# The cosine half of a folded Fourier mixing: rows combined from the tiles just filled instead of a reload, and the turning transfers spread

## The chip, the core and the metric

The kernel runs on one core of a Trainium2 chip. The metric is the device time in microseconds (us) of one execution, from the chip's own clock; several executions give a median. Engines are named as in the profile: PE (TensorE matmul), PEld (its weight loads), DVE (VectorE), ACT (ScalarE), POOL (GpSimd), SP (SyncE, which issues nearly all transfers). "L994" is line 994 of the kernel before; the changed kernel's lines stand about 3 (before the combining) or 24 (behind it) further down.

## What is computed

Two independent things, laid side by side in the output. With S = 2048 and D = 448:

```python
# half A: Fourier mixing with given DFT matrices
a = einsum("bsd,ed->bse", x, dft_hid_re)
b = einsum("bsd,ed->bse", x, dft_hid_im)
y = einsum("ts,bse->bte", dft_seq_re, a) - einsum("ts,bse->bte", dft_seq_im, b)
# half B: attention with 16 heads of 28
q, k, v = split(x_b @ wqkv)
o = softmax(q @ k.T * 28**-0.5) @ v @ wo
out = concatenate([y, o], axis=-1)
```

## The kernel before, in words

**Two streams on one PE.** Attention makes 1024 score tiles of 128x512 (`score`, matmul L1451), whose exponential on ACT (L1455) goes into tiles of the pool `kept_s` (20 tiles of 128x2x512, fp32), and blocks that multiply the exponentials with V (PV, L1462, 32 matmul rows each). All else on PE is filler that goes between scores: projections (L653) first, then the feature transform of half A (`hidden_both`, L886, matmul L908), then the sequence transform in two parts, cosine and sine (`sequence_halved`, matmul L1192), then the output projection (L1686, L1717).

**How the order is made.** A planner in Python (`Schedule`, L124 to L330) writes out the order of all five engines. A task has a key (its due time), a planned duration, tasks that it depends on and slots that it takes from pools. On each engine the ready task with the smallest key is taken; `hold=True` keeps a transfer back until the filler has come to its key. The real engines run their queues in that order, so a waiting instruction holds back all that stand behind it. Three numbers of the planner appear in the change: `RUN` (how many half products, `MZ`, go in a row before something else may), `NOTE_AT` (how early a check's reduction is due) and `FAR_LATE` (how late a store of the far rows is due). Where PE would stand idle in the plan, a score may be emitted twice, to keep PE fed (the repeat writes the same values to the same bank).

**The feature transform.** For each of eight pairs of row tiles, in the order `PAIRS_AT = (7, 0, 6, 1, 5, 2, 4, 3)`, the folded input is split into high and low parts (L873, L879, L881), multiplied (L908), and copied from PSUM into a tile `pair` of `kept_s` by three copies (L504 on DVE or L502 on ACT). `pair` holds for one tile of rows both parts, cosine ([:, 0]) and sine ([:, 1]). It is stored to DRAM, `ab_d` (L917). With rows reversed, it is copied from DRAM to DRAM into `turned_ab` (`turn_rows`, L959: one small copy L974 and four of 32 rows or fewer L969 for each of four groups).

**Combining.** `combine(part, at, after)` (L980) makes the operands of the sequence transform for each part. `group(g)` loads the group's two tiles from `ab_d` into a slot x (L987) and the turned ones into m (L990), casts the low columns of x into `zt` (L994, the z products' operand), makes the sum and difference of the two tiles of x into y (L996) and of m back into x (L998), combines both (L1001) and casts them into the room for `u` (L1003, L1004). `plain(h)` loads a pair of tiles that have no turned partner (L1011) and casts its low columns only (L1015). `combine(0, ...)` is for the cosine part and is called while the feature transform is under way; `combine(1, ...)` is called for the sine part, behind the cosine part's sequence stage.

**Other instructions that stand in the same queues.** `tops(g)` (L1421) makes a product of the first keys (L1435), transposes it on DVE (L1438, which frees its PSUM bank), reduces it (L1439), transposes the result (L1442) and stores it (L1444). The output of a PV block is normalised on DVE (L1517 to L1521) and stored (L1527). Differences of rows for the sequence stage are made on DVE (L1226, L1230, L1235), sums for checks by L1140, L1146 and L1148; weights are loaded by L1164 and L955; q and k by L1313, L1314.

Of the kernel before, what the change touches and what calls it, by code (L numbers as in the profile page):

```python
# [26 lines left out]
NT = S // P  # L27
# [36 lines left out]
NOTE_AT = 5  # L64
# [4 lines left out]
FAR_LATE = 15  # L69
# [3 lines left out]
TURN_LEAD = 18  # L73
# [23 lines left out]
RUN = 8  # L97
# [259 lines left out]
def tile_kernel(ctx, tc, xa, wre, wim, wd, xb, wqkv, wo, out):  # L357
# [461 lines left out]
    def halves(t):  # L819
        return t.rearrange("p (a b) -> p a b", a=2)  # L820
# [67 lines left out]
    def hidden_both(ready):  # L888
        for g in PAIRS_AT:
            x, ld = rows_both(g, fkey(0, 0) - 13)  # L890
            for a in range(2):
# [13 lines left out]
                for b, (seq, o) in enumerate(((seq, fill_s.slot()), (rest, fill_s.slot()))):  # L905
                    for n, (w, i, y, c0, c1, d) in enumerate(seq):
                        def emit(e, w=w, i=i, y=y, c0=c0, c1=c1, o=o, n=n, m=len(seq) - 1):
                            nc.tensor.matmul(o.t[:, c0:c1], of(w, i), y(), start=n == 0, stop=n == m)  # L908
                        last[0] = pe(at, emit, d=d, deps=[last[0], *([h, *ready] if n == 0 else [l] if n == 1 else [])],
                                     use=[hi, lo, o, *low_in, *([pair] if n == len(seq) - 1 else [])])  # L910
                        at += d
                    ways = ((0, 0, EVEN), (1, EVEN, 2 * MAIN)) if b == 0 else ((None, 0, 2 * REST),)
                    for e, c0, c1 in ways:
                        to = lambda pair=pair, e=e: tight(pair.t)[:, :, MAIN:D] if e is None else tight(pair.t)[:, :, e:MAIN:2]
                        ends.append(sch.add({"ACT": 0.43 if e is None else 0.3, "DVE": 0.53 if e is None else 0.32}, key - 10,
                                            lambda w, o=o, to=to, c0=c0, c1=c1: copy_of(w, to(), halves(o.t[:, c0:c1])), deps=[last[0]], use=[o, pair]))
                ab_done[st] = dma(key - 10, lambda pair=pair, st=st: nc.sync.dma_start(  # L917
                    ab_d[st % HT][st // HT].rearrange("b p d -> p b d"), tight(pair.t)), 448, -1.5, deps=ends, use=[pair])

    ab_done, g_at = {}, {}  # L920
# [7 lines left out]
    def z_of(t):  # L928
        return zt()[:, t * LOW:(t + 1) * LOW]
# [29 lines left out]
    def turn_rows(at):  # L959
# [4 lines left out]
        for g in range(FT):  # L964
# [6 lines left out]
            ab_turned[g, 2] = [dma(at(g), lambda n=n, put=put: put(n), 224, 1.5, each=0.75, deps=[ab_done[far], ab_done[far + HT]]) for n in range(4)]  # L971
            if g:
                def first(g=g):
                    nc.sync.dma_start(rows_at(turned_ab[g], 0, [[P * D, 4], [1, D]]), rows_at(ab_d[HT - g], 0, [[P * D, 4], [1, D]]))  # L974
                ab_turned[g, 0] = [dma(at(g), first, 7, 1.5, deps=[ab_done[HT - g], ab_done[NT - g]])]
# [4 lines left out]
    def combine(part, at, after):  # L980
        half = lambda s, i, n=D: tight(s.t)[:, i, :n]
        minus, plus = (ALU.add, ALU.subtract) if part else (ALU.subtract, ALU.add)

        def group(g):
            key = at(g)
            x, y, m = kept_s.slot(), kept_s.slot(), kept_s.slot()
            ld = dma(key, hold=True, emit=lambda: nc.sync.dma_start(tight(x.t), of_rows(ab_d[g], part)),  # L987
                     size=448, extra=0.3, deps=[ab_done[g], ab_done[g + HT]], use=[x])
# [3 lines left out]
            zs = []  # L992
            for j in range(2):
                zs.append(dve(key, lambda j=j: nc.vector.tensor_copy(z_of(g + j * HT), half(x, j, LOW)), 0.26, deps=[ld, *after(g)], use=[x]))  # L994
                z_ready[part, g + j * HT] = zs[j]
            us = [dve_on(key, lambda e, c=c, op=op: e.tensor_tensor(half(y, c), half(x, 0), half(x, 1), op=op), 0.6, deps=[ld], use=[x, y])  # L996
                  for c, op in enumerate((ALU.add, ALU.subtract))]
            ws = [dve_on(key, lambda e, c=c, op=op: e.tensor_tensor(half(x, c), half(m, 0), half(m, 1), op=op), 0.6,  # L998
                         deps=[lm, *us, *zs], use=[x, m]) for c, op in enumerate((ALU.add, ALU.subtract))]
# [8 lines left out]
        def plain(h):  # L1008
            key = at(h) + 1
            x = kept_s.slot()  # L1010
# [810 lines left out]
```

## Time and profile before

| what | us |
|---|---|
| median of three timed runs (lowest, highest) | 798.53 (798.12, 799.5) |
| the profiled execution | 797.17 |
| its span, first to last instruction | 795.4 |
| PE busy | 779.8 (98%) |
| ACT busy | 590.7 (74%) |
| DVE busy | 439.6 (55%) |
| mean granted clock of PE | 0.997 |

The profile shows one execution; the span is 1.77 us shorter than its time. Filler and attention change with the stage: in the trace, projections and values run to about 225 us, the feature transform to about 403, the cosine part to about 575, the sine part to about 705, the output projection to 789. A share of busy time is an average over these stages. A wait in the lists is given as total us, times and the longest, with the instruction that waited and the one that released it.

### The profile page before, as it was taken

What the parts mean: (1) busy time and instruction counts of PE and PEld (TensorE: products, weight loads), DVE (VectorE), ACT (ScalarE), POOL (GpSimd) and SP (SyncE); (2) the same over time, 40 slices, a digit from 0 to 9 for tenths busy, and PEclk for the clock granted to TensorE, in tenths of its full rate; (3) what the DMA queues carried; (4) which work ended last, traced back from release to release, by engine and by line L of the source; (5) the groups of instructions that cost most, each with busy time, mean ns of one, the idle gap of its engine ahead of it and who ended that gap; (6) DMA issues with size and microseconds to landing.
All of it is one profiled execution on the core that took longest, in us unless ns stands there. A gap on an engine that the chain in (4) does not pass through costs nothing.

```text
span 795.4 us, 14120 instructions
## 1 busy us (share of the span) xinstructions
PE 779.8 (98%) x4725; PEld 482.9 (61%) x4725; DVE 439.6 (55%) x928; ACT 590.7 (74%) x1221; POOL 55.9 (7%) x201
## 2 busy tenths in 40 slices
PE   8999999999999989999999999999999999999996
PEld 6886556575556646556566555556555555655576
DVE  6641443362243463444559775679887876673440
ACT  6105877568787868887888878988778888899941
POOL 3000000000000000000011110122011202010000
PEclk9999999999999999999999999999999999999999
DMA  8757876342357554556578875696877849763132
GB/s 297 216 175 236 233 199 215 123 181 102 116 108 223 166 173 135 167 162 208 187 232 244 260 224 169 200 300 180 235 253 245 265 142 290 225 218 116 33 136 86
DMA packets 138610, 152.58 MB, mean 192 GB/s; under 512 B 31140, under 2 KB 109538, under 8 KB 138530
## 3 DMA queue, kind: packets, MB, share of 16 engines
q1 hardware_dynamic: 137810, 150.46, 61.4%
q10 hardware_dynamic: 720, 1.15, 0.4%
q8 instruction: 39, 0.64, 0.4%
q14 instruction: 41, 0.34, 0.1%
HBM read 110.39 MB, written 50.86 MB: 203 GB/s over the span
## 4 chain that ended last, share of the span: by engine, by line
PE 84%; DMA 8%; SPq 3%; ACT 2%; DVE 2%; issue 1%; DVEq 0%
PE bank L1451 29%; PE bank L1462 26%; PE bank L653 11%; PE bank L1192 8%; PE bank L1686 4%; PE bank L908 4%; ACT kept L1455 2%; DMA abd<-kept 1%; DMA kept<-wre 1%; DMA wraw<-wre 1%; DMA k<-qkd 1%; DMA abt<-abd 1%; PE bank L1717 1%; DMA kept<-wqkv 1%; PE bank L1435 1%
## 5 line engine op out<-in xcount | busy, mean ns | idle before, releaser
L1455 ACT ACTIVATE kept<-bank 128x512 f32<-128x512 f32 x1024 | 511.1, 664 | 147.6 <-PE bank L1451 138.1
L1451 PE MATMUL bank<-q,k 85*128 85x512 f32 x1028 | 340.7, 415 | 5.3 <-DVE kept L1438 2.8
L1451 PEld LDWEIGHTS bank<-q,k 85*128 85x128 f32 x1028 | 181.4, 189 | 104.2 <-issue 30.8
L1462 PE MATMUL bank<-kept,v 128*32 128x512 f32 x2048 | 233.0, 595 | 0.0
L1462 PEld LDWEIGHTS bank<-kept,v 128*32 128x32 f32 x2048 | 60.0, 109 | 133.4 <-issue 128.3
L504 DVE COPY kept<-bank 128x226 f32<-128x226 f32 (+3 forms) x64 | 30.8, 503 | 79.2 <-PE bank L908 46.2
L653 PE MATMUL bank<-xt,whi 128*128 128x512 f32 x196 | 69.1, 399 | 1.6 <-DVE xt L498 0.8
L1192 PE MATMUL bank<-zt 128*128 128x226 bf16 x448 | 55.3, 262 | 0.4 <-DVE zt L1226 0.3
L1148 DVE TENSOR_REDUCE diff<-zt 128x1 f32<-128x512 bf16 x73 | 47.7, 677 | 1.1 <-POOL zt L1245 0.7
L1192 PEld LDWEIGHTS <-zt 128*128 128x128 bf16 x448 | 38.4, 99 | 15.0 <-issue 11.3
L653 PEld LDWEIGHTS bank<-xt,whi 128*128 128x128 f32 x196 | 36.4, 188 | 13.7 <-DVE xt L498 1.8
L653 PE MATMUL bank<-xt,wlo 128*128 128x512 f32 x112 | 43.8, 393 | 0.0
L908 PE MATMUL bank<-wd,whi 128*128 128x450 f32 (+3 forms) x128 | 43.0, 381 | 0.0
L653 PE MATMUL bank<-wd,xt 128*128 128x448 f32 x176 | 37.7, 368 | 0.6 <-DVE wd L498 0.6
L1192 PE MATMUL bank<-xt,whi 128*128 128x448 f32 (+1 forms) x128 | 38.2, 326 | 0.0
L653 PEld LDWEIGHTS bank<-wd,xt 128*128 128x128 f32 x176 | 32.7, 188 | 4.6 <-POOL wlo L640 1.0
L1517 DVE STREAM_TRANSPOSE kept<-bank 128x512 f32<-128x512 f32 (+1 forms) x19 | 13.5, 713 | 32.1 <-PE bank L1462 22.7
L504 DVE CAST wd<-bank 128x512 fp32r<-128x512 f32 x12 | 8.3, 691 | 40.6 <-PE bank L653 39.2
L502 ACT ACTIVATE kept<-bank 128x448 f32<-128x448 f32 (+2 forms) x17 | 9.9, 584 | 27.2 <-PE bank L1717 14.8
L1235 DVE TENSOR_TENSOR zt<-wdraw,xraw 128x508 bf16<-128x508 f32 x28 | 19.1, 683 | 17.0 <-PE bank L1192 9.1
L1146 ACT ACTIVATE spent<-zt 128x512 uint8<-128x512 bf16 x39 | 26.0, 666 | 3.3 <-DVE zt L1226 2.0
L1192 PEld LDWEIGHTS bank<-xt,whi 128*128 128x128 f32 x128 | 24.6, 197 | 3.7 <-ACT kept L1455 1.3
(168 smaller groups left out, 742.1 us busy)
## 6 DMA issues: line engine op xcount, KB each, us to landing
wdraw<-wim SPq DMA_DIRECT2D x38, 256.0 KB
qkd<-wd SPq DMA_DIRECT2D x32, 256.0 KB
wdraw<-wre SPq DMA_DIRECT2D x32, 256.0 KB
q<-qkd SPq DMA_DIRECT2D x64, 112.0 KB
k<-qkd SPq DMA_DIRECT2D x64, 112.0 KB
abd<-kept SPq DMA_DIRECT2D x16, 448.0 KB
kept<-abd SPq DMA_DIRECT2D x16, 448.0 KB
qkd<-kept SPq DMA_DIRECT2D x24, 256.0 KB
```

What stands on the lines that cost most here:

```text
L504: nc.vector.tensor_copy(dst, src)
L653: nc.tensor.matmul(o.t[:, :cols], w(), x(), start=(i == 0), stop=(i == n - 1))
L908: nc.tensor.matmul(o.t[:, c0:c1], of(w, i), y(), start=n == 0, stop=n == m)
L1146: nc.scalar.activation(spent, src(), AF.Abs, accum_out=dst)
L1148: nc.vector.tensor_reduce(dst, src(), axis=AX.X, op=ALU.add, apply_absolute_value=True)
L1192: nc.tensor.matmul(o.t[:, at0:at0 + n], cut_of(w.t, e, c), x(), start=first, stop=stop)
L1235: e.tensor_tensor(turned(dl.t, 1, 1, P - 1), mirror(r.t), read(base.t, 1, 1, P - 1), op=minus)
L1451: m = pe(key, lambda e: nc.tensor.matmul(b.t, KT[h][kt // 4].t[:KR + 1, kt % 4 * P:(kt % 4 + 1) * P], q.t[:KR + 1, :], start=True, stop=True),
L1455: return act(key - 20, lambda: nc.scalar.activation(p.t, b.t, AF.Exp, scale=SCALE), deps=[m], use=[b, pair])
L1462: nc.tensor.matmul(o.t[j * VW:(j + 1) * VW, :], VT[h].t[:, kt // 4, kt % 4, :], tiles[i // 2].t[:, i % 2, :], start=(kt < 4 // len(cs)), s ...
L1517: t = dve(key - 20, lambda: nc.vector.transpose(pair.t[:m, 0], o.t[:m]), 0.66, deps=[dep], use=[o, pair], own=RAW_S)
L1686: nc.tensor.matmul(o.t[:, :D], a(), b(), start=(i == 0), stop=(i == 8 and n < N_HELD))
```

## The change

It does four things. (1) In the cosine part, z and the first sums are made straight from the pair tiles that `hidden_both` filled; nothing is loaded from `ab_d` for it. The pair tiles are remembered in `pairs`, and stay taken until the sums have read them and their store has landed. The turned rows are loaded as before, and their sum and difference no longer wait for the sums of the pair. (2) The turning copies are spread by 3 us of due time, due 22 instead of 18 us ahead, planned as 448 instead of 224 KB, and held. (3) The pair's store is planned with 0 instead of −1.5 us extra. (4) `RUN`, `NOTE_AT` and `FAR_LATE` are changed. The sine part combines as before, from reloads.

```diff
-NOTE_AT = 5
+NOTE_AT = 4
-FAR_LATE = 15
+FAR_LATE = 5.0
-TURN_LEAD = 18
+TURN_LEAD = 22
+TURN_STEP = 3.0
+OWN_LEAD = 0.0
+AB_EXTRA = 0.0
-RUN = 8
+RUN = 7
...
+                pairs[st] = pair, ends, key - OWN_LEAD
                 ab_done[st] = dma(key - 10, lambda pair=pair, st=st: nc.sync.dma_start(
-                    ab_d[st % HT][st // HT].rearrange("b p d -> p b d"), tight(pair.t)), 448, -1.5, deps=ends, use=[pair])
+                    ab_d[st % HT][st // HT].rearrange("b p d -> p b d"), tight(pair.t)), 448, AB_EXTRA, deps=ends, use=[pair])
...
-            ab_turned[g, 2] = [dma(at(g), lambda n=n, put=put: put(n), 224, 1.5, each=0.75, deps=[ab_done[far], ab_done[far + HT]]) for n in range(4)]
...
-                ab_turned[g, 0] = [dma(at(g), first, 7, 1.5, deps=[ab_done[HT - g], ab_done[NT - g]])]
+                ab_turned[g, 0] = [dma(at(g) - TURN_STEP, first, 7, 2.5, each=0.6, deps=[ab_done[HT - g], ab_done[NT - g]])]
+            ab_turned[g, 2] = [dma(at(g) + n * TURN_STEP, lambda n=n, put=put: put(n), 448, 1.5, each=0.75, hold=True,
+                                   deps=[ab_done[far], ab_done[far + HT]]) for n in range(4)]
...
+        def own(t, after):
+            pair, ends, key = pairs[t]
+            z_ready[part, t] = dve(key, lambda: nc.vector.tensor_copy(z_of(t), half(pair, part, LOW)), 0.26, deps=[*ends, *after], use=[pair])
+
         def group(g):
...
+            if part == 0:
+                for j in range(2):
+                    own(g + j * HT, after(g))
+                src = [pairs[g + j * HT][0] for j in range(2)]
+                ld = [d for j in range(2) for d in pairs[g + j * HT][1]]
+                of = lambda j: half(src[j], part)
+                zs = []
+            else:
+                of = lambda j: half(x, j)
+                src = [x]
+                ld = [dma(key, hold=True, emit=lambda: nc.sync.dma_start(tight(x.t), of_rows(ab_d[g], part)),
+                          size=448, extra=0.3, deps=[ab_done[g], ab_done[g + HT]], use=[x])]
...
-            us = [dve_on(key, lambda e, c=c, op=op: e.tensor_tensor(half(y, c), half(x, 0), half(x, 1), op=op), 0.6, deps=[ld], use=[x, y])
+            us = [dve_on(key, lambda e, c=c, op=op: e.tensor_tensor(half(y, c), of(0), of(1), op=op), 0.6, deps=ld, use=[*src, y])
...
-                         deps=[lm, *us, *zs], use=[x, m]) for c, op in enumerate((ALU.add, ALU.subtract))]
+                         deps=[lm, *(us if part else ()), *zs], use=[x, m]) for c, op in enumerate((ALU.add, ALU.subtract))]
...
         def plain(h):
             key = at(h) + 1
+            if part == 0:
+                for j in range(2):
+                    own(FT + h + j * HT, after(h))
+                return
```

How the order of the engines moves is shown at three places. `kept`, `bank`, `zt`, `xt` and the like are tiles; the number behind a name tells tiles of one pool apart; `abd` and `abt` are `ab_d` and `turned_ab` in DRAM.

The first place is DVE's queue at the first group of the cosine part, in the middle of the feature transform (about 280 us in the trace of before). Before:

```order
L504 COPY kept_239<-bank_264 128x2x223
L879 TENSOR_SCALAR whi_203<-wraw_200 128x512
L881 SCALAR_TENSOR_TENSOR wlo_204<-wraw_200,whi_203 128x512
L873 TENSOR_TENSOR wraw_200<-kept_226 128x256 x2
L994 CAST zt<-kept_231 128x226 x2
L996 TENSOR_TENSOR kept_243<-kept_231 128x448 x2
L998 TENSOR_TENSOR kept_231<-kept_241 128x448 x2
L1438 STREAM_TRANSPOSE kept_232<-bank_270 128x512
L1001 TENSOR_TENSOR kept_243<-kept_243,kept_231 128x448
L1439 TENSOR_REDUCE kept_232<-kept_232 128x16
```

After (L507 is the copy L504 of before, L1016 the sums L996, L991 the casts to z, L882, L884 and L876 the splits, L1018 the sums of the turned rows L998, L1021 the combining L1001):

```order
L507 COPY kept_229<-bank_265 128x2x223
L1016 TENSOR_TENSOR kept_241<-kept_237,kept_229 128x448 x2
L991 CAST zt<-kept_229 128x226
L882 TENSOR_SCALAR whi_202<-wraw_199 128x512
L884 SCALAR_TENSOR_TENSOR wlo_206<-wraw_199,whi_202 128x512
L876 TENSOR_TENSOR wraw_199<-kept_228 128x256 x2
L507 COPY kept_238<-bank_267 128x2x113
L507 COPY kept_238<-bank_267 128x2x112
L1018 TENSOR_TENSOR kept_231<-kept_245 128x448 x2
L1021 TENSOR_TENSOR kept_241<-kept_241,kept_231 128x448
L1023 CAST xt_193<-kept_241 128x448
```

The casts and the sums stand right behind the copies that fill their tiles; the sums of the turned rows stand by themselves, later, and the transpose of the tops (L1462 there) follows 22 rows behind them.

The second place is SP's queue at the same group. Before:

```order
L1313 DMA k_211<-qkd 56x1x512
L1314 DMA k_211<-qkd 28x512
L990 DMA kept_241<-abt_176 128x2x448
L955 DMA basd_180<-wre 8x15x512
L917 DMA abd_168<-kept_243 128x2x448
L987 DMA kept_231<-abd_168 128x2x448
L1164 DMA xraw<-basd_180 128x2x256 x2
```

After (L973 and L977 are the turning copies L969 and L974 of before, L921 the store L917, L959 the table's turning L955, L1009 the load of turned rows L990):

```order
L973 DMA abt_176<-abd_175 4x32x448
L1468 DMA md_140<-top_252 128x32
L921 DMA abd_168<-kept_237 128x2x448
L973 DMA abt_176<-abd_175 4x32x448 x2
L973 DMA abt_176<-abd_175 4x31x448
L959 DMA basd_180<-wre 8x16x512
L977 DMA abt_177<-abd_175 4x448
L1337 DMA k_211<-qkd 56x1x512
L1338 DMA k_211<-qkd 28x512
L921 DMA abd_168<-kept_229 128x2x448
L959 DMA basd_180<-wre 8x15x512
L1009 DMA kept_245<-abt_176 128x2x448
```

The reload L987 behind the store is gone, and the turning copies stand with other transfers between them. In the whole program there are 8 loads from `abd` of a pair (L987 and L1011) where there were 16.

The third place is PE's queue where the cosine part's filler ends and the sine part's begins (about 570 us in the trace of before). Before:

```order
L1451 MATMUL bank_265<-q_223,k_210 128x512
L1192 MATMUL bank_264<-xt_194,whi_203 128x226
L1192 MATMUL bank_264<-xt_194,wlo_208 128x226
L1451 MATMUL bank_271<-q_220,k_210 128x512
L1451 MATMUL bank_269<-q_221,k_210 128x512
L1451 MATMUL bank_270<-q_222,k_210 128x512
L1451 MATMUL bank_265<-q_223,k_210 128x512
L1451 MATMUL bank_271<-q_220,k_210 128x512 x2
L1451 MATMUL bank_269<-q_221,k_210 128x512 x2
L1192 MATMUL bank_267<-xt_194,whi_203 128x448
```

After, the last eleven rows of the run and the first of the PV block behind it (L1475 is the score, L1486 PV):

```order
L1475 MATMUL bank_268<-q_219,k_212 128x512
L1475 MATMUL bank_270<-q_216,k_212 128x512 x2
L1475 MATMUL bank_271<-q_217,k_212 128x512 x2
L1475 MATMUL bank_266<-q_218,k_212 128x512 x2
L1475 MATMUL bank_269<-q_219,k_212 128x512 x2
L1475 MATMUL bank_268<-q_216,k_213 128x512 x2
L1475 MATMUL bank_270<-q_217,k_213 128x512 x2
L1475 MATMUL bank_264<-q_218,k_213 128x512
L1475 MATMUL bank_271<-q_219,k_213 128x512
L1475 MATMUL bank_266<-q_216,k_213 128x512
L1475 MATMUL bank_269<-q_217,k_213 128x512 x2
L1486 MATMUL bank_268<-kept_243,v_214 32x512 x2
```

A run of eight scores (six and two repeats; a score row with "x2" is a score and its repeat) between products becomes a run of 25 (18 and seven repeats) between two PV blocks, with four scores and another seven z products behind the second.

More of the change, by code (lines that the diff above doesn't have):

```diff
@@ L916, in hidden_both @@
                                             lambda w, o=o, to=to, c0=c0, c1=c1: copy_of(w, to(), halves(o.t[:, c0:c1])), deps=[last[0]], use=[o, pair]))
+                pairs[st] = pair, ends, key - OWN_LEAD
                 ab_done[st] = dma(key - 10, lambda pair=pair, st=st: nc.sync.dma_start(
-                    ab_d[st % HT][st // HT].rearrange("b p d -> p b d"), tight(pair.t)), 448, -1.5, deps=ends, use=[pair])
-    ab_done, g_at = {}, {}
+                    ab_d[st % HT][st // HT].rearrange("b p d -> p b d"), tight(pair.t)), 448, AB_EXTRA, deps=ends, use=[pair])
+    ab_done, g_at, pairs = {}, {}, {}
     u_ready, z_ready, u_last = {}, {}, {}
@@ L986, in group @@
             x, y, m = kept_s.slot(), kept_s.slot(), kept_s.slot()
-            ld = dma(key, hold=True, emit=lambda: nc.sync.dma_start(tight(x.t), of_rows(ab_d[g], part)),
-                     size=448, extra=0.3, deps=[ab_done[g], ab_done[g + HT]], use=[x])
+            if part == 0:
[10 more added lines that the diff above has]
+                          size=448, extra=0.3, deps=[ab_done[g], ab_done[g + HT]], use=[x])]
             lm = dma(key + 1, hold=True, emit=lambda: nc.sync.dma_start(tight(m.t), of_rows(turned_ab[g], part)),
                      size=448, extra=0.3, deps=[d for n in (0, 2) for d in ab_turned[g, n]], use=[m])
[L992 to L996, printed above, removed]
+            if part:
+                zs = []
+                for j in range(2):
+                    zs.append(dve(key, lambda j=j: nc.vector.tensor_copy(z_of(g + j * HT), half(x, j, LOW)), 0.26, deps=[*ld, *after(g)], use=[x]))
+                    z_ready[part, g + j * HT] = zs[j]
+            us = [dve_on(key, lambda e, c=c, op=op: e.tensor_tensor(half(y, c), of(0), of(1), op=op), 0.6, deps=ld, use=[*src, y])
                   for c, op in enumerate((ALU.add, ALU.subtract))]
             ws = [dve_on(key, lambda e, c=c, op=op: e.tensor_tensor(half(x, c), half(m, 0), half(m, 1), op=op), 0.6,
-                         deps=[lm, *us, *zs], use=[x, m]) for c, op in enumerate((ALU.add, ALU.subtract))]
+                         deps=[lm, *(us if part else ()), *zs], use=[x, m]) for c, op in enumerate((ALU.add, ALU.subtract))]
             for c, op in enumerate((plus, minus)):
@@ L1009, in plain @@
             key = at(h) + 1
+            if part == 0:
+                for j in range(2):
+                    own(FT + h + j * HT, after(h))
+                return
             x = kept_s.slot()
```

## The prediction, on record before the run

> **What bounds the kernel now.** I read the head of the page first, then what TensorE (PE) waited for, then the chain of waits around the largest of those waits, and last the same stretch in short windows with the granted clock. The head of the page and the top of PE's waits:
>
> ```profile
> span 795.4 us, 14120 instructions
> PE 779.8 (98%) x4725; PEld 482.9 (61%) x4725; DVE 439.6 (55%) x928; ACT 590.7 (74%) x1221; POOL 55.9 (7%) x201
> ...
> PE bank L1451 <- DVE kept L1438: 2.8, 1, 2.8
> PE bank L1545 <- POOL ident masks.py:199: 1.4, 1, 1.4
> ```
>
> PE is busy in 98% of the span, so what can be won is little: its idle time (795.4 − 779.8 = 15.6 us, much of it the start and the drain), the time in which it runs at a lower clock, and the time in which a row counts as busy but is stretched because ScalarE (ACT) can't empty banks faster. The largest wait of PE in the whole run is a single one of 2.8 us: a score (L1451) that needs a PSUM bank, which the transpose L1438 on VectorE (DVE) frees. The chain of waits through that place:
>
> ```profile
> 274.76 5.69 DMA abd<-kept
> ...
> 280.53 0.03 SPq L987
> ...
> 280.60 3.54 DMA kept<-abd
> ...
> 284.16 0.04 DVE zt L994
> ...
> 284.63 1.08 DVE kept L996 x2
> ...
> 285.73 1.16 DVE kept L998 x2
> 286.89 0.64 DVE kept L1438
> ...
> 287.57 0.73 PE bank L1451 x2
> ```
>
> Read from the bottom: the score waits for L1438; L1438 has nothing to do with the combining, but stands behind L994, L996 and L998 in DVE's queue; L994 stands there waiting for the reload of a pair from DRAM (3.54 us); and that reload waited on SP's queue for the landing of the pair's own store (5.69 us). So a round trip of 9.2 us through DRAM holds a PSUM bank back. PE's timeline and the short windows (per engine busy us and count, then the granted clock, DMA share, GB/s) price it:
>
> ```profile
> 282.82 1.34 PE L1451 MATMUL bank<-q,k 85*128 85x512 f32 x5
> 284.00 0.27 PE L908 MATMUL bank<-wlo,whi 128*128 128x226 f32 x1
> ...
> 287.57 0.73 PE L1451 MATMUL bank<-q,k 85*128 85x512 f32 x2 [2.84 <-DVE kept L1438]
> ```
>
> ```profile
> 284.00:286.00 2.00, 0.73 (x4) 0.30 (x2) 1.80 (x5) 2.00 (x5) 0.20 (x1) 1.00 1.05 335
> 286.00:288.00 2.00, 0.43 (x2) 0.39 (x3) 2.00 (x5) 0.31 (x1) 0.00 (x0) 1.00 0.75 269
> 288.00:290.00 2.00, 2.00 (x11) 1.75 (x10) 1.97 (x7) 1.83 (x4) 0.00 (x0) 0.79 0.35 86
> 290.00:292.00 2.00, 2.00 (x7) 1.72 (x7) 1.42 (x5) 1.64 (x4) 0.00 (x0) 0.50 0.43 109
> 292.00:294.00 2.00, 2.00 (x14) 1.17 (x16) 1.31 (x3) 1.28 (x4) 0.00 (x0) 0.86 0.67 171
> ```
>
> PE stands for 2.84 us, and behind the wait the granted clock is 0.79, 0.50 and 0.86 in three windows of 2 us: 2 x (0.21 + 0.50 + 0.14) = 1.70 us of full-speed work lost. The whole stall costs 2.84 + 1.70 = 4.54 us.
>
> A sentence on the clock from outside the rows: the Trainium skill, "TensorE: Matmul & The Clock Gate", section "Part 1: The HAM clock gate", has the clock halve after at least one idle window of about 3.4 us, the window running freely; taken as a threshold on the gap, a wait of 2.84 us would cost no clock, the saving would be 2.84 and the sum below 1.70 us smaller. The trace shows the half clock after 2.84 us of idling, so the measurement decides, and 1.70 us stands.
>
> **The change part by part.** 1. *No reload in the cosine half.* The casts to z and the two sums of each group now read the pair tiles that were just filled. Four L987 and four L1011 issues of 448 KB go from the SP queue, and with them what L994 waited for and what L987 waited for on SP (a row of the list of waits, then two of SP's own list: us in total, times, longest):
>
> ```profile
> DVE zt L994 <- DMA kept<-abd: 6.4, 3, 3.9
> ...
> SPq L990 <- DMA abt<-abd: 18.0, 5, 5.2
> ...
> SPq L987 <- DMA abd<-kept: 12.8, 4, 5.3
> ```
>
> In the new order the casts and sums stand right behind the copies that fill their tiles, and the next transpose of the kind of L1438 stands over 20 rows behind the last instruction that waits for a load. The 2.84 us wait and its clock loss go: −4.54 us. The other two waits of L994 (6.4 − 3.9 = 2.5 us) had no PE wait behind them in the list above and bring nothing. What is late next at this place is the row pair L998, which still waits for the turned rows that come by store, turning copy and load; it now waits without L996 in front of it. I put it at zero, since L998 began right behind L996 in the chain (its load was there already), and price its failure among the rivals.
>
> 2. *Issues and bytes.* Eight loads less are off the path, since SP's queue stood waiting anyway (18.0 and 12.8 us in the rows above): zero. If the transfers of that stretch get faster by it, nothing but a wait that is already priced gets shorter: zero.
>
> 3. *Turning copies spread, stores planned later.* The copies of a group now go out with 3 us between them in the plan, a lead of 22 instead of 18 and twice the planned size. Their end decides when L990 can load and L998 run. They move behind other loads in the SP queue, and are held until the filler work has come that far. Transfers of this kind took between 3.54 us and the two below, so the plan's margin may fail by some us: zero in the forecast, a rival below.
>
> ```profile
> 343.94 4.88 DMA abd<-kept
> ...
> 349.98 6.91 DMA abt<-abd
> ...
> 356.95 8.78 DMA wraw<-wre
> ```
>
> 4. *The start of the sine half.* This is the price of the change that I can see. The three numbers of the planner (notes, far differences, runs of half products) and the different use of the slots move the filler there. In before, PE had one run of eight scores at this place (six scores and two that are repeated, since the planner puts a repeat where PE has nothing else), then product and score in turn. In the new order there is a run of 25 between two blocks of PV: 18 scores and 7 repeats. A run without filler goes at ACT's pace, once the banks are used up. ACT's timeline and PE's at that place:
>
> ```profile
> 570.87 9.91 ACT L1455 ACTIVATE kept<-bank 128x512 f32<-128x512 f32 x20 [3.01 <-PE bank L1451]
> ```
>
> ```profile
> 573.70 2.96 PE L1451 MATMUL bank<-q,k 85*128 85x512 f32 x8
> 576.50 0.36 PE L1192 MATMUL bank<-xt,whi 128*128 128x448 f32 x1
> ```
>
> An exponential takes 9.91 / 20 = 0.50 us; a score on PE takes (284.00 − 282.82) / 5 = 0.236. PE's excess in the old run was 576.50 − 573.70 − 6 x 0.236 = 1.38 us. In the new one the first six scores find banks (the block of PV ahead gives ACT time to catch up), and the other twelve are paced by ACT: 12 x (0.50 − 0.236) = 3.17 us, in which the 7 repeats (7 x 0.236 = 1.65 us) fit. The difference is 3.17 − 1.38 = +1.8 us. Lower bound: if the planner's repeats are all that is lost, 5 more repeats in the whole program x 0.236 = 1.18 in all; upper bound: all 18 at ACT's pace, 18 x 0.264 − 1.38 = +3.4 us. I take 1.8, from the row of the run that is nearest in kind.
>
> 5. *The start of the cosine half.* A run of nine scores with two repeats appears where there was none: 2 x 0.236 = +0.5 us (between 0, if ACT had to catch up anyway, and the 1.38 of the old run).
>
> 6. *The tail.* With 18 scores drawn forward at one place, 1001 of the scores (repeats counted) are out by the end of the sequence stage, 951 before. The stretch in which ACT was the end of the chain before that point:
>
> ```profile
> 700.92 5.00 ACT kept L1455 x10
> ...
> 706.97 0.50 PE bank L1451
> ```
>
> gets easier, and the output projection keeps fewer runs of six to eight scores (one for four). Between 0 and the 1.38 us that one such run cost: I take −0.5 us.
>
> 7. *Copies from DVE to ACT* (about five) and one sum moved between them: ACT is busy 590.7 of 795.4 us and the move is some 2 us of it, hidden at 74%; zero, or inside part 4 where it isn't hidden.
>
> Sum: −4.54 + 1.8 + 0.5 − 0.5 = −2.74 us. The profiled execution took 797.17 us (span 795.4 and 1.77 around it), so 794.43. The median of the three timed runs is 798.53, 1.36 above the profiled one; the forecast on that scale is 798.53 − 2.74 = **795.8 us**. With the bounds of parts 4 to 6 it lies between 794.2 and 797.
>
> **The rivals.** (a) *The runs cost nothing.* If ACT's time ahead of schedule in the long run is given back in full later, parts 4 and 5 vanish and the time is 798.53 − 4.54 − 0.5 = 793.5 us. For it: the number of exponentials is the same, and scores drawn forward leave PE's later filler free. Against it: PE is the bound over the span, and an ACT-paced run is PE time that no later stage returns. Chance 0.17.
>
> (b) *The wait comes back at the turned rows: no change.* L998 is now the first DVE instruction of the group that waits for DRAM; behind it stand splits of the weights, copies that free banks and the transposes. If its turned rows come as late as L990's longest wait on SP (5.2 us in the rows above), PE stands again for about the 2.84 us: 795.8 + 2.84 = 798.6 us without a clock loss, 800.3 with one of 1.70. For it: 18.0 us of SP's waiting is for the turning copies, and these are now spread out. Against it: the longer lead, and L998 found its rows ready in before. Chance 0.20.
>
> (c) *Slower, at the start of the sine half.* All four groups and the plain casts of the sine half now stand on DVE ahead of the next differences that feed PE. One group with its plain casts took 576.95 − 571.16 = 5.79 us on DVE:
>
> ```profile
> 571.16 0.46 DVE L994 CAST zt<-kept 128x226 bf16<-128x226 f32 x2
> ...
> 576.95 0.41 DVE L1083 CAST xt<-kept 96x512 fp32r<-96x512 f32 x1
> ```
>
> Two groups and about 1 us of other work stand between the products around the long run, 12.6 us; PE's cover is that run (6 x 0.236 + 12 x 0.50 = 7.4), two blocks of PV of 3.6 us as below, and eight scores (1.9): 16.5 us. A margin of 3.9 us.
>
> ```profile
> 278.67 3.64 PE L1462 MATMUL bank<-kept,v 128*32 128x512 f32 x32
> ```
>
> It decides from the point where the reloads (which the sine half still makes) are late by more than that: one that takes 8.78 instead of 3.54 us is late by 5.2 and costs 1.3 us; two in a row are late by 10.5 and cost 6.6. Halfway, 4 us, with the clock loss of 1.70, gives 795.8 + 5.7 = 801.5 us. For it: each reload is in front of everything on an in-order queue, and that stretch is rich in transfers. Against it: two late transfers must meet. Chance 0.13.
>
> **How the numbers follow.** The forecast has 0.50, (a) 0.17, (b) 0.20, (c) 0.13. A measurement of this kernel can tell about 0.2%, 1.6 us: faster is below 796.9, slower above 800.1. Faster: 0.45 of the forecast and (a)'s 0.17, 0.61 with rounding down for the upper edge. Same: the rest of the forecast and most of (b), 0.23. Slower: (c) and the part of (b) with a clock loss, 0.16. The range reaches from within (a), 792.4, to the top of (b), 800.4, and leaves out (c) and the lower part of (a), under 2 in 10.
>
> **What would show it right or wrong.** In the changed profile the wait of a score for the transpose of the tops should be gone from the top of PE's waits, and the granted clock should be 1.00 from 284 to 296 us; SP should hold four loads of pairs where it held eight, and no cast of the cosine half should wait for a load. The run of 25 should show as some 7.4 us of scores with ACT behind ACT without a gap. A PE wait on DVE in the feature stage with a chain over turning copies is (b); a PE wait of over 2 us for z or differences near 570 to 600 us is (c). If the long stall is gone and the time is still within 0.2%, part 4 was mis-sized; if PE's rows show neither wait nor stretch there, it is (a).

## The result, and the profile after

| kernel | median us (lowest, highest; runs) | ratio to before, 95% interval |
|---|---|---|
| before | 798.53 (796.99, 801.14; 6) | |
| after | 793.25 (792.91, 794.62; 6) | 0.9929 [0.9907, 0.9951] |

The change makes the kernel 5.3 us faster. The forecast was −2.7 us, to 795.8; the time lies inside its range, and next to rival (a)'s 793.5. The profiled executions differ by less than the medians: 797.17 before, 793.73 after, −3.4 us. The head of the page of after and the top of PE's waits:

```profile
span 791.9 us, 14113 instructions
PE 780.8 (99%) x4730; PEld 481.0 (61%) x4730; DVE 440.2 (56%) x921; ACT 593.0 (75%) x1227; POOL 54.9 (7%) x201
...
PE bank L1569 <- POOL ident masks.py:199: 1.4, 1, 1.4
PE bank L656 <- ACT xt L595: 1.1, 1, 1.1
```

The wait of 2.8 us for the transpose of the tops is gone; PE's longest wait is now one at the start of the program. The windows at the place where it was (columns as in the prediction):

```profile
284.00:286.00 2.00, 2.00 (x12) 1.64 (x10) 1.69 (x6) 2.00 (x6) 0.00 (x0) 1.00 0.36 86
286.00:288.00 2.00, 2.00 (x11) 1.60 (x11) 1.90 (x5) 2.00 (x6) 0.00 (x0) 1.00 0.55 171
288.00:290.00 2.00, 2.00 (x19) 0.64 (x21) 0.65 (x2) 2.00 (x6) 0.00 (x0) 1.00 0.54 135
290.00:292.00 2.00, 2.00 (x21) 0.48 (x13) 0.00 (x0) 0.61 (x2) 0.00 (x0) 1.00 0.83 277
```

PE is busy throughout and the granted clock stays at 1.00, as it does up to 296 us. DVE's, SP's and PE's timelines at the other two places that the prediction speaks of:

```profile
278.36 1.16 DVE L1018 TENSOR_TENSOR kept<-kept 128x448 f32<-128x448 f32 x2 [3.06 <-ACT kept L1479]
```

```profile
272.91 0.36 SPq L1009 DMA_DIRECT2D kept<-abt  x1
```

```profile
579.23 7.31 PE L1475 MATMUL bank<-q,k 85*128 85x512 f32 x25
586.47 3.64 PE L1486 MATMUL bank<-kept,v 128*32 128x512 f32 x32
```

The sums of the turned rows (L1018) do wait, 3.06 us, and for their load, although the row names ACT. The wait on DVE's queue ahead of them begins at 274.62 us and takes 3.59 us; the last landing of the load, issued by L1009 at 272.91, is in the trace at 278.18 us, and the exponential that the row names is one of an unbroken row of them on ACT. So the turned rows are late here, as rival (b) has it, and PE doesn't stop for it: the copies of the pair, which free banks, stand ahead of these sums on DVE. The run of 25 scores takes 586.47 − 579.23 = 7.24 us (forecast 7.4). So the stall is gone and the long run is there, as the prediction has it. Whether the first came from the missing reload is what the experiments ask.

### The profile page after: what moved, and what is told of

It is laid out like the page before. It is cut to its first block, busy times and chain, and to the rows that moved or that the text cites. A ratio compares the mean times of both kernels' runs of the same rounds, so it can differ in the third digit from the quotient of the medians.

```text
span 791.9 us, 14113 instructions
## 1 busy us (share of the span) xinstructions
PE 780.8 (99%) x4730; PEld 481.0 (61%) x4730; DVE 440.2 (56%) x921; ACT 593.0 (75%) x1227; POOL 54.9 (7%) x201
## 4 chain that ended last, share of the span: by engine, by line
PE 95%; SPq 2%; DMA 2%; DVE 0%; issue 0%; ACT 0%; DVEq 0%
PE bank L1475 33%; PE bank L1486 29%; PE bank L656 11%; PE bank L1216 9%; PE bank L911 5%; PE bank L1710 4%; PE bank L1741 1%; PE bank L1459 1%; DMA kept<-xb 1%; DMA qb<-qkd 1%; SPq L1337 1%; PE bank L1559 0%; PE bank L1135 0%; SPq L1338 0%; DMA q<-md 0%
## 5 line engine op out<-in xcount | busy, mean ns | idle before, releaser
L1475 PE MATMUL bank<-q,k 85*128 85x512 f32 x1033 | 344.0, 416 | 1.0 <-DMA q<-md 0.9
L1475 PEld LDWEIGHTS bank<-q,k 85*128 85x128 f32 x1033 | 180.8, 189 | 100.4 <-issue 32.1
L1486 PE MATMUL bank<-kept,v 128*32 128x512 f32 x2048 | 233.0, 595 | 0.0
L1486 PEld LDWEIGHTS bank<-kept,v 128*32 128x32 f32 x2048 | 60.0, 109 | 134.3 <-issue 129.8
L507 DVE COPY kept<-bank 128x226 f32<-128x226 f32 (+4 forms) x59 | 27.8, 493 | 76.5 <-PE bank L911 53.3
L656 PEld LDWEIGHTS bank<-xt,whi 128*128 128x128 f32 x196 | 36.3, 188 | 13.4 <-ACT kept L1479 1.7
L505 ACT ACTIVATE kept<-bank 128x448 f32<-128x448 f32 (+3 forms) x22 | 12.9, 599 | 26.0 <-PE bank L1741 14.6
L507 DVE CAST wd<-bank 128x512 fp32r<-128x512 f32 x12 | 8.3, 691 | 40.6 <-PE bank L656 34.0
L1541 DVE STREAM_TRANSPOSE kept<-bank 128x512 f32<-128x512 f32 (+1 forms) x19 | 13.5, 713 | 30.6 <-PE bank L1486 22.1
L1462 DVE STREAM_TRANSPOSE kept<-bank 128x512 f32<-128x512 f32 (+1 forms) x20 | 14.2, 709 | 26.7 <-PE bank L1459 25.7
```

Source lines behind the costliest of these rows:

```text
L507: nc.vector.tensor_copy(dst, src)
L656: nc.tensor.matmul(o.t[:, :cols], w(), x(), start=(i == 0), stop=(i == n - 1))
L1462: r = dve(key, lambda o=o, mt=mt: nc.vector.transpose(mt.t[:32 * n, 0], o.t[:32 * n]), 0.64, deps=[m], acq=[mt], use=[o], own=RAW_S)
L1475: m = pe(key, lambda e: nc.tensor.matmul(b.t, KT[h][kt // 4].t[:KR + 1, kt % 4 * P:(kt % 4 + 1) * P], q.t[:KR + 1, :], start=True, stop=True),
L1486: nc.tensor.matmul(o.t[j * VW:(j + 1) * VW, :], VT[h].t[:, kt // 4, kt % 4, :], tiles[i // 2].t[:, i % 2, :], start=(kt < 4 // len(cs)), s ...
```

## The experiments

Line numbers in the experiments' profiles shift by some lines with their edits; the names of tiles tell which instruction is meant. All medians below are of executions on the chip of the runs of before beside them; the ratio stands with its interval, and is not quite the quotient of the two medians.

| kernel | median us | before beside it | ratio, 95% interval |
|---|---|---|---|
| one transpose moved (top_first) | 792.24 | 798.12 | 0.9914 [0.9885, 0.9944] |
| after, again | 793.45 | 798.12 | 0.9932 [0.991, 0.9954] |
| after without the 7 repeats | 795.04 | 798.12 | 0.9956 [0.9934, 0.9978] |
| combining alone | 799.7 | 798.12 | 1.0029 [0.9997, 1.0061] |
| combining alone, qb ahead | 802.35 | 796.93 | 1.0066 [1.0036, 1.0096] |
| the same, turned rows' sums later | 796.22 | 797.02 | 0.9995 [0.9976, 1.0014] |
| after, turning copies as before | 801.16 | 796.93 | 1.0045 [1.0019, 1.0071] |
| after, reload put back | 793.13 | 796.93 | 0.9952 [0.9935, 0.9968] |
| after, three numbers as before | 795.51 | 796.93 | 0.998 [0.9964, 0.9997] |
| before, turning part alone | 794.88 | 797.02 | 0.9981 [0.9964, 0.9998] |
| before, store's number alone | 801.64 | 797.02 | 1.0056 [1.0033, 1.0078] |
| before, again (one profile) | 797.69 | 797.02 | |

**One transpose moved.** The plan of before is kept, and one instruction is written out earlier:

```diff
+                if t.tag == "late":
+                    parked.append((t, e))
+                else:
+                    t.emit(e)
+                if t.tag == "top":
+                    while parked:
+                        x, w = parked.pop(0)
+                        x.emit(w)
...
+            if part == 0 and g == 0:
+                for t in (*zs, *us, *ws):
+                    t.tag = "late"
...
+            r.tag = "top"
```

> The kernel before with a single instruction moved: the transpose of the tops (L1438) stands ahead of the first group's casts and sums (L994, L996, L998) on VectorE; nothing else changes place on any engine. Theory A (the gain is the one stall, 2.84 us of waiting and 1.70 us of clock, behind the reload): 798.5 - 4.5 = 794.0 us or a ratio of about 0.9943, the wait of a score for that transpose gone and the clock 1.00 from 284 to 296 us, although the reload still takes its 9.2 us. Theory B (the gain comes from the bytes saved, the spread copies or the other order of the filler): the time stays at 798.5 within 1.6 us, because the wait moves to the next instruction that needs the reload.

Measured: 792.24 us, ratio 0.9914. On DVE, the transpose now stands in the time in which the reload is waited for:

```profile
282.47 0.72 DVE L1449 STREAM_TRANSPOSE kept<-bank 128x512 f32<-128x512 f32 x1 [2.73 <-PE bank L1446]
283.69 0.47 DVE L1002 CAST zt<-kept 128x226 bf16<-128x226 f32 x2 [0.50 <-DMA kept<-abd]
```

The reload and its bytes are still there, DVE still waits for it (0.50 us behind the transpose), and the gain is all there. Theory A holds: what cost time was a transpose behind a waiting cast, not the reload. Beside the same runs of before this is 1.2 us below the changed kernel, which has the long run of scores and this one has not.

**After, again.** The same file as after.

> The changed kernel once more, on the chip of the three runs it is compared with: 793.25 us within 0.8 us, ratio to before 0.993. No theory differs here; it is the yardstick for the run without repeats.

Measured: 793.45 us, as expected.

**Combining alone.** Before, with only the cosine half's combining changed; the diff is that of `own`, `group`, `plain` and `pairs` above.

> The kernel before with the cosine half combined from the filled tiles and nothing else of the change: turning copies, planned sizes and the planner's three numbers as before. The order has its long run of scores at the start of the sine half here too (24 with 10 repeats), another of 10 with 3 repeats. Theory A: the stall is gone and the runs cost a little more than in the changed kernel, 793.5 to 795.5 us. Theory B (the spread copies and the numbers are needed): the turned rows come late, VectorE waits in front of the sums of the turned rows, and a stall of 2 us or more of TensorE shows in the feature stage, 796 to 799 us.

Measured: 799.7 us, no gain, and a wide spread (796.14 to 807.94). The chain of waits and the windows behind it in its profile:

```profile
265.30 8.40 DMA qb<-qkd
...
273.84 0.47 PE bank L1455
```

```profile
274.00:276.00 2.00, 2.00 (x8) 1.57 (x8) 1.58 (x3) 1.10 (x3) 0.00 (x0) 0.63 0.87 281
276.00:278.00 2.00, 2.00 (x6) 1.59 (x5) 1.26 (x4) 2.00 (x5) 0.00 (x0) 0.50 0.89 269
...
282.00:284.00 2.00, 2.00 (x6) 1.74 (x6) 0.73 (x3) 0.84 (x2) 0.00 (x0) 0.50 0.37 122
284.00:286.00 2.00, 2.00 (x11) 1.78 (x10) 1.93 (x5) 1.08 (x3) 0.00 (x0) 0.81 0.30 115
```

The old stall is gone, and another has its place: the product of the tops waits 2.6 us for its rows of q (qb), which SP issued behind five turning copies and which took 8.40 us to land; the clock is at half from about 274.5 to 284.8 us. Theory B's time, by a mechanism that neither theory named. In before the load of qb, issued at 265.92 us, stands behind the same five copies too; but there the product that needs it comes at 282.58 us, and here it is due 11 us earlier.

**Combining alone, qb ahead.** In the kernel just told, the load of qb is written out ahead of the copies, nothing else moves:

```diff
+AHEAD_OF = (2, 2)
...
+        for t in (*ab_turned[0, 2], *ab_turned[1, 0]):
+            t.tag = "late"
...
+            if (g, c) == AHEAD_OF:
+                lq.tag = "ahead"
```

> The kernel with the combining part of the change alone (runs of scores, turning copies and numbers as in that experiment), in which one load on SP is moved: the rows of q for the tops (qb) go out ahead of the five turning copies of the first group instead of behind them; nothing else changes place. Theory A (that kernel is slow because qb is queued behind the burst of turning copies: 8.40 us to land where TensorE waits for it, and the half clock behind the wait): the wait of 2.6 us is gone, the granted clock 0.998 or more, 793 to 795 us. Theory B (the turned rows or the long runs are what costs): still 797 us or more, with the clock under 0.997.

Measured: 802.35 us: no better. The wait for qb is gone and the next one stands behind it, in DVE's and PE's timelines:

```profile
277.55 1.16 DVE L1027 TENSOR_TENSOR kept<-kept 128x448 f32<-128x448 f32 x2 [5.25 <-DMA kept<-abt]
```

```profile
282.15 0.80 PE L1486 MATMUL bank<-q,k 85*128 85x512 f32 x1 [4.04 <-DVE kept L514]
282.87 6.41 PE L1497 MATMUL bank<-kept,v 128*32 128x512 f32 x32
```

The sums of the turned rows wait 5.25 us for their load; a copy that frees a bank stands behind them, PE stops for 4.04 us, and the block of PV behind it takes 6.41 us where it takes 3.64 at full clock. This is the mechanism of rival (b), with a longer wait of PE than the 2.84 us priced there, in a kernel that has part 1 without part 3.

**The same, turned rows' sums later.** On DVE the copies of the next pair and its cast are written out ahead of those sums and what follows from them:

```diff
+            if t == 6:
+                z_ready[part, t].tag = "copied"
...
+                if part == 0 and g == 0:
+                    for t in (*ws, u, a, b):
+                        t.tag = "turned"
```

> The kernel with the combining part alone and qb moved ahead of the copies, in which one more thing is moved, on VectorE only: the three copies that fill the next pair and its cast stand ahead of the first group's sums of turned rows and what follows from them (eight rows), instead of behind them; nothing else changes place. Theory A (what is left of the loss there is the sums of turned rows waiting for their load, 5.25 us in that kernel, in front of copies that free a bank): the wait of 4.0 us and the half clock behind it go, 794 to 796 us. Theory B (combining from the tiles costs elsewhere, for instance in the 10 repeats of its long run): 798 us or more without such a wait.

Measured: 796.22 us, 6 us less (on another chip; against before, 0.9995 in place of 1.0066). The top of PE's waits and the window that holds it:

```profile
PE bank L1490 <- ACT kept L1494: 1.4, 1, 1.4
```

```profile
280.00:290.00 10.00, 8.62 (x54) 5.58 (x46) 6.84 (x17) 8.07 (x18) 0.21 (x1) 1.00 0.55 174
```

A wait of 1.4 us is left, and the clock stays at 1.00. The expectation was 794 to 796, just missed. Two moves by hand, one load on SP and eight rows on DVE, undo the stalls of the two kernels just told; the long runs of scores are left, and against before nothing is won.

**After, turning copies as before.** The turning part of the diff above is undone (`TURN_LEAD`, `TURN_STEP`, size, `hold`), and with it the store's number `AB_EXTRA`; all else stays.

> The changed kernel with the turning copies and the pair's store planned as before (not spread, lead 18, not held), all else of the change in place. The order puts the five copies in a row ahead of the load of qb again. Theory A (the spread matters because of what the burst holds back): a wait of TensorE for qb near 270 us and a spread of times as in the kernel with the combining alone, 797 to 802 us. Theory B (the spread is worth nothing): 793 to 794.5 us.

Measured: 801.16 us. PE's list has the wait for qb again, and the clock falls behind it:

```profile
PE bank L1458 <- DMA qb<-qkd: 2.3, 1, 2.3
```

```profile
270.00:275.00 5.00, 2.66 (x17) 1.51 (x10) 2.02 (x5) 0.14 (x1) 0.00 (x0) 0.88 0.47 154
275.00:280.00 5.00, 5.00 (x15) 4.08 (x14) 3.88 (x9) 4.49 (x9) 0.00 (x0) 0.50 0.86 271
280.00:285.00 5.00, 5.00 (x19) 4.38 (x18) 2.32 (x7) 2.72 (x5) 0.21 (x1) 0.60 0.32 103
```

Theory A. Without the spread and the store's number the change is a loss of 4 us against before.

**After, reload put back.** `combine` as before, all else of the change in place.

> The changed kernel with the reload of the pairs in the cosine half put back, all else of the change in place. The order again has a transpose of the tops behind a cast that waits for the reload. Theory A (reload in front of the transpose is the stall): a wait of a score for that transpose of 1 to 4 us, a clock of 0.997 or less, 796.5 to 800 us. Theory B (the spread copies and numbers carry the gain): 793 to 794.5 us.

Measured: 793.13 us, as fast as the changed kernel (ratios to before of 0.9952 here and 0.9932 there, on two chips; their intervals overlap). Theory A failed here, though the transpose stands between the two casts from the reload. DVE's timeline says why:

```profile
281.25 0.27 DVE L999 CAST zt<-kept 128x226 bf16<-128x226 f32 x1
283.04 0.72 DVE L1443 STREAM_TRANSPOSE kept<-bank 128x512 f32<-128x512 f32 x1 [1.52 <-PE bank L1440]
```

and SP's its reload:

```profile
277.26 0.36 SPq L992 DMA_DIRECT2D kept<-abd  x1
```

The first cast waits for nothing. SP issued the reload at 277.26 us, not at 280.60, and DVE comes to the cast at 281.25, when it has landed. In this order the reload isn't late, so that it stands in front of a transpose costs nothing. Why it isn't late stands under "Before, turning part alone".

**After, three numbers as before.**

```diff
-NOTE_AT = 4
+NOTE_AT = 5
...
-FAR_LATE = 5.0
+FAR_LATE = 15
...
-RUN = 7
+RUN = 8
```

> The changed kernel with the planner's three numbers as before (NOTE_AT 5, FAR_LATE 15, RUN 8). The order keeps qb ahead of the spread copies and has 24 scores with 10 repeats and 10 with 3 repeats near the start of the sine half. Theory A (the numbers only shift filler): no stall, 793 to 795 us, longer than the changed kernel by the further 6 to 8 repeats at most (1.4 to 1.9 us). Theory B (the numbers carry the gain): 796 us or more.

Measured: 795.51 us, some 2 us more than the changed kernel, with no stall. PE's timeline:

```profile
569.86 6.82 PE L1475 MATMUL bank<-q,k 85*128 85x512 f32 x24
576.61 3.64 PE L1486 MATMUL bank<-kept,v 128*32 128x512 f32 x32
...
593.39 3.49 PE L1475 MATMUL bank<-q,k 85*128 85x512 f32 x10
596.72 0.95 PE L1216 MATMUL bank<-zt 128*128 128x226 bf16 x8
```

Two runs without filler: 6.75 us for 14 scores and 3.33 us for 7, less 21 x 0.236 leaves 5.1 us of excess, where the changed kernel's one run has 7.24 − 18 x 0.236 = 3.0. The difference of 2.1 us is about the time measured.

**Before, turning part alone.** `TURN_LEAD`, `TURN_STEP`, size and `hold` of the diff above; reload, store and numbers as before.

> The kernel before with the turning part of the change alone (spread by 3 us, lead 22, planned as 448 KB, held); reload, the store's planned number and the planner's three numbers as before. The order keeps the copies in a row ahead of qb, and the transpose of the tops stands behind the reload's casts and sums, as before. Theory A (the order around the reload decides, not the spread itself): the stall stays, with a lower clock behind it, 797 to 800 us. Theory B (the spread shortens the transfers that are waited for): 793 to 795.5 us.

Measured: 794.88 us, faster by 2.1 us, or 1.5 by the ratio (theory B's range). The stall is gone although reload and transpose stand in the old order:

```profile
280.04 0.47 DVE L996 CAST zt<-kept 128x226 bf16<-128x226 f32 x2 [1.01 <-DMA kept<-abd]
280.41 1.16 DVE L998 TENSOR_TENSOR kept<-kept 128x448 f32<-128x448 f32 x2
281.48 0.71 DVE L1440 STREAM_TRANSPOSE kept<-bank 128x512 f32<-128x512 f32 x1
```

The cast waits 1.01 us where it waited 3.87, and the transpose is early enough. SP's queue says why the reload comes earlier. In before:

```profile
273.54 0.38 SPq L990 DMA_DIRECT2D kept<-abt  x1
...
274.76 0.40 SPq L917 DMA_DIRECT2D abd<-kept  x1
```

and here:

```profile
271.27 0.38 SPq L918 DMA_DIRECT2D abd<-kept  x1
271.69 0.47 SPq L992 DMA_DIRECT2D kept<-abt  x1
...
276.21 0.46 SPq L989 DMA_DIRECT2D kept<-abd  x1
```

In before the pair's store stands behind the load of the turned rows (L990), which holds the queue until the turning copies have landed and a slot is free, at about 273.6 us; so the store goes out at 274.76 and the reload, which waits for its landing, at 280.60. Here the store stands ahead of that load, and the reload goes out at 276.21. It is so in "reload put back" too (store 269.10, load of the turned rows 274.26, reload 277.26). No run moved that store alone.

The rest of the change's gain is missing. The long run of this order, 23 scores with 9 repeats, begins at 570.49 us and the block of PV behind it at 577.22; that is 577.22 − 570.49 − 14 x 0.236 = 3.4 us of excess, only 0.4 more than the changed kernel's; "reload put back", which has the store's number and the planner's three numbers besides, is the one that has the rest.

**Before, store's number alone.**

```diff
-                    ab_d[st % HT][st // HT].rearrange("b p d -> p b d"), tight(pair.t)), 448, -1.5, deps=ends, use=[pair])
+                    ab_d[st % HT][st // HT].rearrange("b p d -> p b d"), tight(pair.t)), 448, 0.0, deps=ends, use=[pair])
```

> The kernel before with one planned number changed: the store of a pair is planned with 0 instead of -1.5 us extra, as in the changed kernel. Reload, turning copies and the planner's three numbers are as before. By itself it puts qb ahead of the turning copies, the reload's casts behind one more VectorE instruction, and a long run of 23 scores with 9 repeats at the start of the sine half. Theory A (the stall comes from transfers that the plan believes in earlier than they land; any honest number there removes it): no wait of TensorE over 1.5 us in the feature stage, 793.5 to 796.5 us. Theory B (the reload has to go, or the copies to be spread): a wait for the transpose of the tops of 1 to 4 us is left, 797 us or more.

Measured: 801.64 us, slower; both theories missed the place. PE's waits, and the chain at the new one:

```profile
PE bank L1451 <- ACT kept L1455: 3.4, 1, 3.4
...
PE bank L1451 <- DVE kept L1438: 1.0, 1, 1.0
```

```profile
355.21 9.29 DMA wraw<-wre
...
364.52 0.79 DVE zt L1226 x2
...
365.88 0.19 ACT spent L1146
366.06 0.49 ACT kept L1455
...
366.60 0.74 PE bank L1451 x2
```

The stall at 284 us has shrunk to 1.0 us (the store stands ahead of the load of the turned rows here as well, and the reload goes out at 277.35), and one of 3.4 us stands 80 us later. A load of the sequence matrix goes out behind another group's turning copies, takes 9.29 us, a difference on DVE waits for it, a sum on ACT waits for the difference, and the exponentials stand behind the sum. A more cautious number for one transfer moved the order, and another transfer became the late one.

**After without the 7 repeats.**

```diff
-                            t.emit("PE")
+                            again += 1
+                            if again < 3:
+                                t.emit("PE")
```

The first two repeats of the program, at the start of the cosine half, stay.

> The changed kernel without the seven repeats in the run of 25 scores; the order is the same otherwise. Theory A (ScalarE paces the run at 0.50 us a score, the repeats lie in time that is lost anyway): the run still takes 7.2 to 7.4 us, the time is the changed kernel's within 0.5 us. Theory B (the repeats cost TensorE time): 7 x 0.236 = 1.65 us faster. Theory C (they keep the clock up): TensorE is idle by 1.65 us in small gaps, the granted clock falls behind the run and the time is up to 1.7 us longer.

Measured: 795.04 us, 1.6 us longer: theory C. The run and the block behind it in PE's timeline, then two windows:

```profile
579.07 7.37 PE L1477 MATMUL bank<-q,k 85*128 85x512 f32 x18
586.36 4.41 PE L1488 MATMUL bank<-kept,v 128*32 128x512 f32 x32
```

```profile
584.00:586.00 2.00, 2.00 (x6) 1.16 (x5) 1.92 (x4) 2.00 (x6) 0.00 (x0) 0.63 0.22 57
586.00:588.00 2.00, 2.00 (x9) 0.40 (x12) 2.00 (x5) 2.00 (x6) 0.00 (x0) 0.51 0.76 244
```

The run takes as long with 18 matmuls as with 25, 7.29 against 7.24 us, so the repeats are free. Without them the clock falls to half in a stretch that the page counts as busy throughout, and PV takes 4.41 instead of 3.64 us. This profiled execution, at a mean clock of 0.997, took 793.11 us and is the fastest of the twelve; their median clock is 0.995, so most of them lose more clock than it shows.

**Before, again.** The same file as before, for a second profile.

> The kernel before once more, for another profile of its stall. If the clock behind the wait falls for one window of 3.4 us whatever the wait (theory A of the prediction's sum), the loss is 1.7 us again; if it is a matter of the execution (theory B), the wait or the stretch at half clock has another length, which would account for the 25 and 30 timed executions of this kernel having mean clocks from 0.989 to 1.000 and times from 792.7 to 804.3 us.

Measured: 797.69 us at a mean clock of 0.992. PE's wait and three windows:

```profile
PE bank L1451 <- DVE kept L1438: 3.0, 1, 3.0
...
280.00:285.00 5.00, 3.07 (x18) 1.65 (x10) 2.29 (x6) 3.54 (x7) 0.20 (x1) 0.95 0.97 314
285.00:290.00 5.00, 3.91 (x12) 3.35 (x13) 4.19 (x10) 2.35 (x5) 0.00 (x0) 0.50 0.45 129
290.00:295.00 5.00, 5.00 (x19) 3.10 (x21) 2.79 (x6) 3.40 (x7) 0.00 (x0) 0.53 0.39 105
```

The wait is nearly the same (3.02 against 2.84 us), and the clock is at half for three times as long, from about 284.5 us: 5 x (0.05 + 0.50 + 0.47) = 5.1 us, some 0.8 of it inside the wait itself, against 1.70. Theory B. Even so this execution took only 0.5 us longer than the first (797.69 against 797.17), so not every us of lost clock was a us of time.

## Why the prediction was right, and where it was wrong

**Right: the stall, and that it bounds.** One in-order wait on DVE held a bank back, and taking it away gives the gain: one moved row alone gives ratio 0.9914. It is gone in the changed kernel.

**Undersized: the clock term.** 1.70 us was what one execution showed. Over the 84 executions of before that ran beside the experiments the median of the mean granted clock is 0.995; over the 14 of after it is 0.999. That is about 0.004 x 794 = 3.2 us of clock, and not 1.70; as a time it is an upper estimate, by the two profiles of before. It fits that the profiled execution (797.17, clock 0.997) was 1.36 below the median: it was one with a short stretch at half clock. The 15 executions of before with a clock of 0.9965 or more have a median of 794.84 us, the 17 below 0.993 one of 798.59. Four of the 84, at a clock of 0.999 or more, took 791.97 to 793.37 us, as little as the changed kernel; so the stall itself may be missing in some executions, which no profile shows. With the larger term the sum is −2.84 − 3.2 + 1.2 (the next point) = −4.8 us; measured were −5.3 and, for the second set of runs, −4.7.

**Nearly right: the runs of scores.** The ends that parts 4 to 6 give for themselves, added up, reach from about 793.8 to 798.8 us, and not from 794.2 to 797 as the prediction has it. Part 4 forecast 7.42 us for the run of 25 and 3.17 of excess; measured 7.24 and 3.0. Parts 4 to 6 together were to cost 1.8 us; the changed kernel is 1.2 us above the one with before's filler and the transpose moved, if that is all that tells the two apart. The difference of the two runs being 3.0 − 1.38 = 1.6, a remainder of −0.4 is left for parts 5 and 6 together, not told apart. Rival (a), nearest in time, is then wrong in its mechanism: the run is paid for, and the time came so near because the stall had cost more than was forecast.

**Wrong: which part takes the stall away.** Step 1 put −4.54 us on the missing reload and step 3 put the spread copies at zero. The runs showed nearly the reverse. With the spread and the reload (reload put back) the time is 793.13; with the combining and no spread it is 801.16 or, alone, 799.7; the spread alone gains (794.88). Combining alone does take the old stall away, as step 1 says, but it brings a new one. That the forecast still had the way and the range right is in part luck: the part that it credited gives no gain by itself, and parts that it put at zero or counted as cost are needed.

The step that failed is "L998 began right behind L996 in the chain (its load was there already)". It was there because in that order DVE came to L998 only at 285.73 us, 12 us after the load went out (273.54). Where the sums of the pair wait for no reload, DVE comes to the sums of the turned rows 10 to 13 us earlier: at 272.3 us in "qb ahead" and at 275.3 in the changed kernel, and waits 5.25 and 3.06 us for their load (rival (b)'s condition).

Whether PE stops depends on what stands behind them: in "qb ahead" a copy that frees a bank does, in the changed kernel such copies stand ahead, as the rows of the first place above show. The other new wait is PE's own, for qb (8.40 us to land). With the combining and no spread PE's order has the product that needs it 8.4 us (273.46 − 265.03, "turning copies as before") after its issue; in the changed kernel that product comes at 293.40 us, 35 us after the issue at 258.01. By these times it matters little that qb also goes out ahead of the copies there; no run tried it, but in "turning part alone" qb goes out behind them and no wait for it comes. Where the reload stays and the old stall goes or shrinks, the pair's store stands ahead of the load of the turned rows on SP.

**Wrong: the numbers as mere cost.** The three numbers of the planner take about 2 us out of the filler in the changed order, since the old ones give two runs without filler there. Why the three numbers move the runs so was not followed.

**Right: rival (c) did not come.** No wait of PE near 570 to 600 us is in after's list.

**Left open.** Which of lead, step, planned size and hold in the turning part removes the stall was not tried apart, and in the changed kernel the turning part was not undone without the store's number.

## What to carry to other kernels

Where queues run in order, ask not how long a transfer takes, but which instruction that others need stands behind the one that waits for it; moving that one row can be worth as much as removing the transfer. When a wait is removed, list the other transfers that landed in its shadow, with their own latencies, before calling them early. And price a stall from several executions: the clock behind it may vary more than the wait.

## What the runs showed of the hardware

Behind a wait of PE, or from within it, the granted clock fell to half for one, two or three times 3.41 us, by the traces' own records of the clock, and the length did not go by the length of the wait: 3.41 us behind a wait of 2.84 (before); 6.83 behind 3.4 (store's number alone) and 4.04 (qb ahead); 10.24 behind 2.3 (turning copies as before), 2.6 (combining alone) and 3.0 (before, again). Behind 1.4 us (the same, turned rows' sums later) it did not fall. The clock also halves where PE never stands still for long: in the run without repeats, with one score of 0.236 us in every 0.4 to 0.5, it is at half for 3.41 us. The Trainium skill, "TensorE: Matmul & The Clock Gate", section "A second HAM failure mode: psum-queue depth-cycling", tells of such a loss from short idling between groups of matmuls; this run agrees, with a clock of 0.63 and 0.51 in two windows and 1.6 us.
